# Bringing w_out in through the GpSimd DMA queue, cast to bf16 on the way

## The chip, the cores and the metric

The kernel runs on one core of one Trainium2 chip. The metric is the device time of one execution in microseconds (us). The core has five engines that run side by side: PE (TensorE, matrix multiplication), DVE (VectorE), ACT (ScalarE), POOL (GpSimd) and SP (SyncE, which here only issues DMAs). Sixteen DMA engines move data between HBM and the on-chip memory SBUF. PE writes its sums to PSUM, a small memory of eight banks.

## The reference

Sliding-window attention with a few global keys, followed by a feed-forward layer with softplus. Four sequences of 768 rows, 8 heads of 64; 96 local keys and 8 global ones; a feed-forward layer from 512 to 2048 and back.

```python
scores = scale * np.matmul(q, k.transpose(0, 1, 3, 2))
keep = is_global | is_local
scores = scores - slopes[:, None, None] * dist[None, :, :]
scores = np.where(keep, scores, -1000000000.0)
a = np.exp(scores - np.max(scores, axis=-1, keepdims=True))
a = a / (np.sum(a, axis=-1, keepdims=True) + 1e-09)
x = np.matmul(a, v)                        # heads side by side: 3072 x 512
h = x @ w_in                               # 512 x 2048
g = np.maximum(h, 0.0) + np.log1p(np.exp(-np.abs(h)))
return g @ w_out                           # 2048 x 512, float32
```

All inputs are float32 in HBM: q, k and v 6.3 MB each, w_in and w_out 4.2 MB each.

## The kernel before

**Tiles.** The 3072 rows are 24 blocks of 128 rows; two neighbouring blocks form a unit, for which q, k and v are loaded together (0.5 MB each). Two blocks also form a group of 256 rows in the feed-forward layer, so there are 12 units and 12 groups.

**Attention of a block n, in two parts of four heads.** q and k are cast to bf16 (`cast_q`, L718, or `cast_rows`, L737) and transposed, for the first three units on PE through PSUM (`transp_pe`, L803), later by transposing DMAs (`transp_dma`, L837). `scores` (L874) multiplies them into PSUM. For blocks in `PE_BIAS` PE first writes the distance bias into the bank (a seed, L887); for the others DVE adds it (`z`, L932). ACT takes the exponential into `pb` (L939), PE multiplies by v (L956), DVE divides by the row sum (L966, L967), and the result is transposed into `XT` (L986 to L998). From the third block of a sequence on, POOL copies the global keys and values beside the local ones (L854, L863).

**Feed-forward of a group g.** `mm1` (L1004) works in eight slots p of eight matmuls each: a slot needs both `XT` halves and its columns of `w_in_bf`. ACT takes exp (L1028, `e`) and ln(1 + e) (L1039, `g`). `mm2` (L1055) multiplies g by `w_out_bf`; a matmul with 256 rows of w_out needs piece p of eight. DVE copies the sum out and SP stores it.

**Weights.** `load_w` (L693) brings w_in and w_out in eight pieces of 0.5 MB each: SP issues a DMA into a float32 buffer of a ring of 12 (`raw`, L710), and an engine named in `ENG_W` casts it into `w_in_bf` or `w_out_bf` (L712). A raw buffer can be filled again only when its casts are done. A w_in piece holds half of the rows of 512 columns, so a slot waits for two pieces; pieces whose column index stands in `NARROW` hold all rows of 256 columns, so a slot waits for one.

**Order.** All operations are handed to a planner (L24 to L186), which is run when the program is built. It knows an estimated duration for each operation and each DMA, gives every operation a due time, worked backwards from the matmuls (`due`, L66, plus a shift from the table `NUDGE`), and plays the machine forward (`run`, L79), each engine taking the most urgent operation that is ready. The order that results is fixed for each engine. `FIRST_LOADS` (L190) is the order in which the raw buffers of the first three units and of the weights are handed out. Where PE would idle at the beginning, up to 90 matmuls on a blank tile are put in (`filler`, L1171); they compute nothing that is used.

**Queues.** SP issues nearly all DMAs, in one order; ACT issues q of the first unit and one store. POOL issues none. A DMA also waits until the one eight before it in the plan is done. In the order built, SP's loads stand as k0, v0, q1, k1, w_in 3, v1, w_in 1, 2, 7, 0, 6, 5, 4, q2, w_out 0, k2, v2, w_out 1, 3, 2, 4, 6, 7, 5 (k1's second half follows w_in 3), and then those of the fourth unit.

Of the kernel before, what the change touches and what calls it, by code (L numbers as in the profile page):

```python
# [23 lines left out]
class Planner:  # L24
# [54 lines left out]
    def run(self, first=0.7, dma_first=1.0, dma_last=1.4, fixed=None, stretch=None):  # L79
# [40 lines left out]
        while True:  # L120
# [50 lines left out]
            while events and events[0][0] <= now + 1e-9:  # L171
                _, _, kind, o = heapq.heappop(events)
                if kind == "free":
                    free[o.eng] = True
                    if o.work:
                        queues[o.eng].append([o, o.work * stretch(o), now + dma_first])
                    else:
                        o.end = now
                        tell([u for u in o.users if u.eng == o.eng])
                        push(now + o.lat, "done", o)  # L180
                else:
                    o.done = True
                    tell([u for u in o.users if o.work or u.eng != o.eng])
# [6 lines left out]
FIRST_LOADS = "v0 k0 q0 i3 i1 q1 o0 v1 k1 i0 i2 i7 i4 o1 i6 q2 k2 i5 o5 o2 o3 o7 v2 o6 o4".split()  # L190
LOAD_LEAD = 2.5
LEADS = {3: 2.25, 4: 2.75, 5: 3, 6: 2.75, 7: 2.75, 8: 3.5, 9: 2.25, 10: 2.75, 11: 3.5}
FILLERS = 90
TABLE_RANK = -9000.0
BIAS0_ON = ["ACT", "DVE"]
BIASA_ON = ["ACT"]
PE_BIAS = (0, 1, 3)
PE_KEYS = {
    0: (("s", 1, 0), ("s", 1, 1), ("h1",), ("o",)),
    1: (("s", 0, 0), ("s", 0, 1), ("s", 1, 0), ("s", 1, 1)),  # L200
    2: (("s", 1, 0), ("x",), ("s", 0, 0), ("s", 0, 1)),
}
PE_X = {0: ("h0",), 1: ("h0",), 2: ("o",), 3: ("o",), 4: ("x",), 5: ("x",)}
PV_KEYS = {
    (0, 0): ("o",),
    (0, 1): ("o",),
    (1, 0): ("o",),
    (1, 1): ("h1",),
# [6 lines left out]
    (0, 0): ("s", 0, 0),  # L215
# [7 lines left out]
NARROW = (0,)  # L223
TAIL = 8.0
ENG = {
    0: {"k": ["POOL", "DVE"], "q": ["POOL", "ACT"], "tk": ["DVE", "ACT"], "tq": ["DVE", "DVE"], "v": ["POOL"]},
    1: {"k": ["DVE", "POOL"], "q": ["POOL", "DVE"], "tk": ["ACT", "DVE"], "tq": ["DVE", "DVE"], "v": ["POOL", "DVE"]},
    2: {"k": ["ACT", "DVE"], "q": ["POOL", "POOL"], "tk": ["DVE", "DVE"], "tq": ["DVE", "DVE"], "v": ["POOL", "ACT"]},
}
ENG_X = {0: "DVE", 1: "ACT", 2: "DVE", 3: "DVE", 4: "ACT", 5: "ACT"}  # L230
ENG_W = {
    "i0": "DVE",
    "i1": "POOL",
    "i2": "POOL",
    "i3": "DVE",
    "i4": "POOL",
    "i5": "POOL",
    "i6": "POOL",
    "i7": "POOL",
    "o0": "POOL",  # L240
    "o1": "POOL",
    "o2": "DVE",
    "o3": "POOL",
    "o4": "POOL",
    "o5": "POOL",
    "o6": "POOL",
    "o7": "POOL",
# [3 lines left out]
    "a0.1": -1,  # L251
    "a0.2": 2,
    "a0.5": 1,
    "a0.6": -1,
    "a0.7": 0.5,
    "a1.0": -2,
    "a1.1": -1,
    "a1.3": -2,
    "a1.4": -2,
    "a1.5": 4,  # L260
    "a1.6": 2,
# [3 lines left out]
    "b0.0.0": 8,  # L265
    "b0.0.10": 0.5,
    "b0.0.14": 0.5,
    "b0.0.4": 0.5,
    "b0.0.6": -8,
    "b0.0.8": -1,  # L270
    "b0.1.0": 1,
    "b0.1.10": 1,
    "b0.1.12": 1,
    "b0.1.2": -8,
    "b0.1.8": -8,
    "b1.0.0": -0.5,
# [3 lines left out]
    "b1.0.2": -1,  # L280
# [7 lines left out]
    "biasFalse0": -1,  # L288
    "biasFalse1": -2,
    "biasFalse2": 0.5,  # L290
    "biasFalse3": -2,
    "biasFalse4": -2,
    "biasFalse5": 4,
    "biasFalse6": -4,
    "biasFalse7": -2,
    "biasTrue0": 1,
    "biasTrue1": -4,
    "biasTrue3": 2,
    "biasTrue4": 4,
    "biasTrue6": 0.5,  # L300
    "biasTrue7": 2,
    "castk0.1": -8,
    "castk1.0": 1,
    "castk1.1": 4,
    "castk2.0": 8,
    "castk2.1": 1,
    "castk3.00": -0.5,
    "castk3.10": -0.5,
# [3 lines left out]
    "castq0.0": 1,  # L312
    "castq0.1": 0.5,
    "castq1.1": -1,
    "castq2.0": -4,
    "castq2.1": 8,
    "castq4.0": 8,
    "castv0.00": -4,
    "castv0.11": -0.5,
    "castv1.00": -8,  # L320
    "castv1.01": 2,
    "castv1.11": -2,
    "castv2.00": 0.5,
    "castv2.01": -0.5,
    "castv2.10": 8,
    "castv2.11": -8,
# [5 lines left out]
    "cin1": 2,  # L332
    "cin2": -1,
    "cin3": 4,
    "cin4": -2,
    "cout0": -2,
    "cout1": 1,
    "cout3": -0.5,
    "cout5": -1,
    "cout6": -4,  # L340
    "cpk0.0": -1,
    "cpk0.1": 2,
    "cpk1.0": 0.5,
    "cpk2.1": 1,
    "cpq0.0": 0.5,
    "cpq0.1": 8,
    "cpq1.0": 1,
    "cpq2.0": 0.5,
    "cpq2.1": 8,
    "d0": 0.5,  # L350
    "d0e": 2,
    "dl0a": 2,
    "dl0b": 0.5,
    "dl0c": 8,
    "dl1a": 8,
    "dl1c": 8,
    "e0.1": 4,
    "e0.3": 2,
    "e0.5": 1,
    "e0.7": -8,  # L360
    "e1.0": -8,
    "e1.2": 8,
    "e1.4": -8,
    "e1.5": -1,
    "e1.6": -4,
# [4 lines left out]
    "ex1.0": 1,  # L370
    "ex1.1": -1,
    "ex2.0": -2,
    "ex3.1": 8,
    "ex4.1": -1,
    "ex5.0": -0.5,
    "ex5.1": 1,
    "gk5": -8,
    "gk7": 0.5,
    "gv4.0": -0.5,
    "gv4.1": 8,  # L380
    "gv5.0": 1,
    "gv5.1": 2,
    "gv6.0": -8,
    "gv6.1": 4,
    "gv7.0": 2,
    "gv8.0": -8,
    "gv8.1": -0.5,
    "ldk0.0": 1,
    "ldk0.1": -1,
    "ldk1.0": 8,  # L390
    "ldk1.1": -0.5,
    "ldk2.0": 2,
    "ldk4": 8,
    "ldk5": 0.5,
    "ldq0.0": -0.5,
    "ldq0.1": 8,
    "ldq1.0": 2,
    "ldq2.0": 0.5,
    "ldq2.1": 2,
    "ldq3": -4,  # L400
    "ldv1": 8,
    "ldv2": 8,
    "ldv4": 0.5,
# [3 lines left out]
    "ln0.0": -1,  # L407
    "ln0.1": 1,
    "ln0.3": -2,
    "ln1.0": 2,  # L410
    "ln1.1": 0.5,
    "ln1.3": -4,
    "nm0.0": -0.5,
    "nm0.1": -1,
    "nm1.0": -0.5,
    "nm2.1": -1,
    "nm3.0": 0.5,
    "nm4.0": 0.5,
    "nm4.1": -0.5,
    "nm5.0": -4,  # L420
    "nm5.1": 8,
# [3 lines left out]
    "oc0.1.0": -0.5,  # L425
    "oc1.0.0": 2,
    "ones": 4,
    "pv0.1": -8,
    "pv1.0": -8,
    "pv1.1": -1,  # L430
    "pv2.0": -2,
    "pv3.0": -1,
    "pv4.1": 8,
    "pv5.0": 8,
    "pv5.1": 8,
    "pv6.0": -1,
    "pv6.1": -4,
    "sb1.0": 1,
    "sb1.1": -0.5,
    "sb2.0": -2,  # L440
    "sb3.0": -2,
    "sb4.0": 1,
    "sb4.1": -4,
    "sc0.1": -4,
    "sc1.0": 8,
    "sc1.1": 0.5,
    "sc2.0": -0.5,
    "sc3.0": -8,
    "sc4.0": -0.5,
# [5 lines left out]
    "st0.1.0": -1,  # L455
    "st1.0.0": -4,
    "table": -1,
    "trk0.0": -8,
    "trk2.0": 0.5,
    "trk2.1": 2,  # L460
    "trk3": 0.5,
    "trk4": -2,
    "trq0.0": -4,
    "trq1.0": -0.5,
    "trq1.1": -2,
    "trq2.0": 2,
    "trq3": -0.5,
    "trq4": 8,
    "win0": 8,
    "win1": 8,  # L470
    "win2": -1,
    "win3": -2,
    "win4": -2,
    "win5": 8,
    "win6": 0.5,
    "win7": -8,
# [6 lines left out]
    "xc0": 2,  # L483
    "xc1": 8,
    "xc2": -1,
    "xc3": -2,
    "xc4": -1,
    "xc5": -4,
    "xt1": -1,
    "xt2": 1,  # L490
    "xt3": 2,
    "xt4": 1,
    "xt5": 0.5,
    "z4.0": 1,
    "z4.1": 0.5,
# [4 lines left out]
DIST0_ON = "ACT"  # L500
# [10 lines left out]
    (4, 1): 1,  # L511
    (5, 0): 1,
    (5, 1): 1,
    (6, 0): 0,
    (6, 1): 1,
    (7, 0): 1,
    (7, 1): 0,
}
T0 = 11.0
LATER = 55.0  # L520
MARGIN = {-1: 10.5, 0: -15.0, 1: 69.0, 2: 65.5, 3: 21.0}
SOONER = {"cin": -20.0, "cout": -25.0}
LAST_KEYS = (("s", 0, 0), ("x",), ("o",))
WHOLE = (0, 4, 6, 7, 8, 9, 10, 12, 13, 14, 15, 16, 17, 18, 23)
LOAD_ON = {"q0": "ACT"}


@with_exitstack
def kernel(
# [122 lines left out]
    def raw_slot(name):  # L652
        raw_of[name] = len(raw_of) % NRAW
        return raw_of[name]
# [38 lines left out]
    def load_w(which, p, rank, eng):  # L693

        slot = raw_slot((which, p))
        half, c = p % 2, p // 2
        raw = raw_t[slot][:].rearrange("p (a c) -> p a c", a=2)
        cost, issue = (1.37, 86.0), 0.45
        if which == "in" and c in NARROW:
            raw = raw_t[slot][:].rearrange("p (a c) -> p a c", a=NM)  # L700
            src = moe_w_in[:, W * p : W * p + W]
            dst = w_in_bf[:, :, W * p : W * p + W]
            cost, issue = (1.51, 51.0), 1.05
        elif which == "in":
            src = moe_w_in[W * half : W * half + W, 512 * c : 512 * c + 512]
            dst = w_in_bf[:, 2 * half : 2 * half + 2, 512 * c : 512 * c + 512]
        else:
            src = moe_w_out[W * p : W * p + W, :]
            dst = w_out_bf[:, 2 * p : 2 * p + 2, :]
        op(f"w{which}{p}", "SP", issue, rank, lambda: nc.sync.dma_start(raw, src.rearrange("(a p) c -> p a c", p=P)),  # L710
           writes=raw_keys(slot), dma=cost)
        op(f"c{which}{p}", eng, t_copy(eng, 1024, True), rank, lambda: copy_on[eng](dst, raw),  # L712
           reads=raw_keys(slot), writes=[("w" + which, p)], port=eng == "DVE")
# [71 lines left out]
    def kt_of(n):  # L785
        return kt_unit(unit_of(n))[:, n % 2, :, :]
# [86 lines left out]

    def scores(n, parts, rank):  # L874
# [70 lines left out]
    def pv(n, part, key, rank):  # L945
        i = blocks[n][1]
        u_all = 2 if i else 1
        pb, xs = pb_t[(2 * n + part) % NPB], xs_t[n % NXS]
# [4 lines left out]
        def mm():  # L953
            for h in range(4):
                for u in range(u_all):
                    nc.tensor.matmul(  # L956
                        xv[:, h, :], pb[:, u_all * (2 * (h % 2) + h // 2) + u, :],
                        vb_of(prev if u else n)[:, 4 * part + h, :], start=u == 0, stop=u == u_all - 1,
                    )

        reads = [("pb", (2 * n + part) % NPB), "ones"] + v_keys(n) + (v_keys(prev) if i else [])
# [232 lines left out]
    def attend(n, rank):  # L1194
# [4 lines left out]
        for parts in ((0, 1),) if n in WHOLE else ((0,), (1,)):  # L1199
            scores(n, parts, rank + 0.1 * parts[0])  # L1200
            for part in parts:
                soften(n, part, rank + 0.1 * part)
# [137 lines left out]
```

The softmax here doesn't subtract the row's maximum and nothing guards it: scores larger than these inputs give would overflow.

## Time and profile before

| what | value |
|---|---|
| runs | 222.47, 222.72, 223.34, 222.39 us |
| median | 222.59 us |
| the profiled execution | 222.47 us, of which 220.4 us is the span of the engines' work |
| DMA bytes | 40.96 MB in 220.4 us; HBM read 27.26 MB, written 6.29 MB |
| first feed-forward matmul (L1013) | starts at 22.88 us |
| casts of w_out (L712) | POOL x7, 1042 ns each; DVE x1, 682 ns |
| w_out DMA (L710), issue by SP | x8, median 440 ns |

The span runs from the first to the last instruction of the engines; what lies around it (222.47 - 220.4 = 2.07 us) belongs to the start and the end of the execution. In the profile an engine followed by q (SPq, POOLq) is its queue that issues DMAs and waits. PEld is the loading of weights into PE, beside its multiplications. In a timeline a bracket behind an instruction tells how long the engine had been idle and what ended that.

### The profile page before, as it was taken

What the parts mean: (1) busy time and instruction counts of PE and PEld (TensorE: products, weight loads), DVE (VectorE), ACT (ScalarE), POOL (GpSimd) and SP (SyncE); (2) the same over time, 40 slices, a digit from 0 to 9 for tenths busy, and PEclk for the clock granted to TensorE, in tenths of its full rate; (3) what the DMA queues carried; (4) which work ended last, traced back from release to release, by engine and by line L of the source; (5) the groups of instructions that cost most, each with busy time, mean ns of one, the idle gap of its engine ahead of it and who ended that gap; (6) DMA issues with size and microseconds to landing.
All of it is one profiled execution on the core that took longest, in us unless ns stands there. A gap on an engine that the chain in (4) does not pass through costs nothing.

```text
span 220.4 us, 5042 instructions
## 1 busy us (share of the span) xinstructions
PE 214.5 (97%) x2034; PEld 151.1 (69%) x2062; DVE 111.2 (50%) x204; ACT 160.1 (73%) x216; POOL 92.4 (42%) x156
## 2 busy tenths in 40 slices
PE   8999999999999999999999999999999999999994
PEld 5877896666676876667667757756657777767554
DVE  6469466644676567338447348347448642001121
ACT  5553999936889798678788688678689678887300
POOL 4557776788461576913962402126602220000000
PEclk9999999999999999999999999999999999999999
DMA  5999999999999798999993241999921222011112
GB/s 199 322 346 379 382 360 384 290 266 226 253 237 233 202 239 211 205 247 291 135 183 106 51 141 54 184 248 301 164 60 51 48 74 71 3 48 48 42 57 95
DMA packets 70359, 40.96 MB, mean 186 GB/s; under 512 B 30144, under 2 KB 62272, under 8 KB 70336
## 3 DMA queue, kind: packets, MB, share of 16 engines
q1 hardware_dynamic: 69904, 40.05, 71.9%
q10 hardware_dynamic: 432, 0.59, 0.9%
q8 instruction: 16, 0.26, 0.5%
q14 instruction: 7, 0.06, 0.1%
HBM read 27.26 MB, written 6.29 MB: 152 GB/s over the span
## 4 chain that ended last, share of the span: by engine, by line
PE 82%; DMA 11%; ACT 3%; SPq 2%; issue 1%; DVE 0%; ACTq 0%
PE h_ps L1013 35%; PE o_ps L1062 30%; PE s_ps L1062 5%; PE s_ps L906 5%; PE x_ps L956 5%; DMA raw<-in_moe_w_in_dram 4%; DMA raw<-in_k_dram 4%; DMA raw<-in_v_dram 3%; PE x_ps L1062 2%; SPq L710 2%; ACT e L1028 1%; ACT g L1039 1%; SPq L675 1%; ACT vb L754 1%; ACT kb L730 0%
## 5 line engine op out<-in xcount | busy, mean ns | idle before, releaser
L1013 PE MATMUL h_ps<-XT,w_in_bf 128*128 128x256 bf16 x768 | 95.8, 273 | 0.4 <-ACT e L1028 0.2
L1013 PEld LDWEIGHTS <-w_in_bf 128*128 128x128 bf16 x768 | 72.8, 98 | 17.4 <-issue 0.4
L1028 ACT ACTIVATE e<-h_ps 128x512 f32<-128x512 f32 x96 | 60.0, 630 | 31.7 <-PE h_ps L1013 31.3
L1062 PE MATMUL o_ps<-w_out_bf,g 128*128 128x512 bf16 (+1 forms) x296 | 74.1, 371 | 1.2
L1062 PEld LDWEIGHTS <-g 128*128 128x128 bf16 x416 | 37.4, 98 | 29.4
L932 DVE TENSOR_TENSOR z<-s_ps,biasA 128x1024 f32<-128x1024 f32 x36 | 43.2, 1217 | 17.8 <-PE s_ps L906 11.2
L1039 ACT ACTIVATE g<-e 128x1024 bf16<-128x1024 f32 x48 | 50.7, 1057 | 1.4
L939 ACT ACTIVATE pb<-z 128x1024 bf16<-128x1024 f32 (+1 forms) x42 | 41.1, 987 | 4.1 <-DVE z L932 4.0
L754 POOL CAST kb<-raw 64x512 bf16<-64x512 f32 x36 | 23.2, 645 | 24.2 <-DMA raw<-in_k_dram 22.9
L863 POOL COPY vb<-vb 4x512 bf16<-4x512 bf16 x32 | 20.0, 625 | 30.8 <-PE x_ps L956 29.9
L754 POOL CAST vb<-raw 64x512 bf16<-64x512 f32 x44 | 27.3, 621 | 13.2 <-DMA raw<-in_v_dram 11.4
L1091 DVE COPY osb<-o_ps 128x512 f32<-128x512 f32 (+1 forms) x20 | 13.4, 670 | 38.3 <-PE o_ps L1062 38.0
L956 PEld LDWEIGHTS <-pb 128*128 128x128 bf16 x352 | 16.6, 98 | 5.8
L966 DVE RECIPROCAL rcp<-x_ps 128x4 f32<-128x4 f32 x40 | 7.1, 178 | 23.2 <-PE x_ps L956 23.0
L967 DVE TENSOR_TENSOR xs<-x_ps,rcp 128x256 bf16<-128x256 f32 x40 | 17.0, 424 | 1.4
L956 PE MATMUL x_ps<-vb,pb 128*128 128x65 bf16 x304 | 15.9, 193 | 0.0
L1174 PE MATMUL x_ps<-blank 128*128 128x256 bf16 x90 | 14.3, 318 | 1.1 <-DVE blank L1113 1.1
L1062 PE MATMUL s_ps<-w_out_bf,g 128*128 128x512 bf16 (+1 forms) x62 | 13.1, 351 | 0.1
L1174 PEld LDWEIGHTS <-blank 128*128 128x128 bf16 x90 | 9.8, 115 | 3.6 <-DVE blank L1113 1.1
L906 PEld LDWEIGHTS <-kT 64*128 64x128 bf16 x224 | 6.8, 94 | 6.1 <-issue 5.7
L906 PE MATMUL s_ps<-qT,kT 64*128 64x128 bf16 x224 | 10.5, 218 | 0.0
L712 POOL CAST w_out_bf<-raw 128x1024 bf16<-128x1024 f32 x7 | 7.3, 1041 | 3.3 <-DMA raw<-in_moe_w_out_dram 3.3
(72 smaller groups left out, 105.0 us busy)
## 6 DMA issues: line engine op xcount, KB each, us to landing
raw<-in_v_dram SPq DMA_DIRECT2D x12, 512.0 KB, 5.5
out_dram<-osb SPq DMA_DIRECT2D x23, 256.0 KB, 2.6
raw<-in_q_dram SPq DMA_DIRECT2D x9, 512.0 KB, 5.2
raw<-in_k_dram SPq DMA_DIRECT2D x9, 512.0 KB, 5.3
raw<-in_moe_w_in_dram SPq DMA_DIRECT2D x8, 512.0 KB, 9.8
raw<-in_moe_w_out_dram SPq DMA_DIRECT2D x8, 512.0 KB, 9.1
raw<-in_k_dram SPq DMA_DIRECT2D x6, 256.0 KB, 6.3
raw<-in_q_dram SPq DMA_DIRECT2D x4, 256.0 KB, 8.4
```

What stands on the lines that cost most here:

```text
L754: copy_on[eng](dst, src)
L863: nc.gpsimd.tensor_copy(vb_of(prev)[sl, :, 0:D], vb_of(first)[sl, :, 0:D])
L906: nc.tensor.matmul(reg if unit_of(n) in WIDE else reg.rearrange("p (r t) -> p r t", r=2), kt[rows, 2 * part + m, :], qv(rows, 2 * part + m ...
L932: nc.vector.tensor_tensor(z, src, bias, ALU.add)
L939: nc.scalar.activation(pb[:, 0:nr, :].rearrange("p (y a) b -> p y (a b)", y=2), src, AF.Exp, scale=1.0 / root_d)
L956: nc.tensor.matmul(xv[:, h, :], pb[:, u_all * (2 * (h % 2) + h // 2) + u, :], vb_of(prev if u else n)[:, 4 * part + h, :], start=u == 0, s ...
L967: nc.vector.tensor_tensor(xs[:, 4 * part : 4 * part + 4, :], xv[:, :, 0:D], rcp[:][:, :, None].to_broadcast([P, 4, D]), ALU.mult,)
L1013: last = nc.tensor.matmul(hv[:, j, :], w_in_bf[:, m, fb * P : fb * P + P], XT[g % NXG][:, m, :], start=(m == 0), stop=(m == NM - 1),)
L1028: nc.scalar.activation(e[:, p % 2, :, :].rearrange("p j (b t r) -> p (j b) r t", b=2, r=2), hb[:].rearrange("p (a r t) -> p a r t", a=4, r=2),
L1039: nc.scalar.activation(gt[:, 2 * p - 2 : 2 * p + 2, :].rearrange("p a t -> p (a t)"), e[:].rearrange("p a j t -> p (a j t)"), AF.Ln, bias=1.0,
L1062: nc.tensor.matmul(bank(key)[:, 0 : z - a], gt[:, fb, ns * P : ns * P + P], w_out_bf[:, fb, a:z], start=(fb == 0), stop=(fb == NFB - 1),)
L1174: nc.tensor.matmul(x_ps[:, 0:256], blank[:, 0:P], blank[:, 0:256])
```

## The change

The eight loads of w_out no longer go through raw buffers. POOL issues a DMA whose source is float32 rows in HBM and whose destination is the bf16 tile `w_out_bf`, so that the DMA engines convert. The eight SP issues, the eight casts and the eight turns in the ring of raw buffers are gone. The planner's clock has a longer start for a DMA that POOL issues (1.8 us added), 0.55 us for its issue and 1.55 us for its work.

```diff
-                        queues[o.eng].append([o, o.work * stretch(o), now + dma_first])
+                        queues[o.eng].append([o, o.work * stretch(o), now + dma_first + 1.8 * (o.eng == "POOL")])
...
-        slot = raw_slot((which, p))
         half, c = p % 2, p // 2
-        raw = raw_t[slot][:].rearrange("p (a c) -> p a c", a=2)
+        slot = None
+        if which == "in" or p not in CAST_OUT:
+            slot = raw_slot((which, p))
+            raw = raw_t[slot][:].rearrange("p (a c) -> p a c", a=2)
...
+        if which == "out" and p in CAST_OUT:
+            op(f"cout{p}", "POOL", 0.55, rank, lambda: nc.gpsimd.dma_start(dst, src.rearrange("(a p) c -> p a c", p=P)),
+               writes=[("wout", p)], dma=(1.55, 86.0))
+            return
...
+CAST_OUT = (0, 1, 2, 3, 4, 5, 6, 7)
```

With it come other settings of the plan: the order of the first loads, which engine casts what, which blocks get their bias on PE, in which PSUM banks things stand, and many entries of `NUDGE` (not shown).

```diff
-FIRST_LOADS = "v0 k0 q0 i3 i1 q1 o0 v1 k1 i0 i2 i7 i4 o1 i6 q2 k2 i5 o5 o2 o3 o7 v2 o6 o4".split()
+FIRST_LOADS = "q0 v0 k0 i3 k1 q1 o5 i2 k2 i1 o3 v1 i7 o7 i6 o0 o1 q2 i4 o6 i0 o4 o2 v2 i5".split()
-BIAS0_ON = ["ACT", "DVE"]
+BIAS0_ON = ["DVE"]
-PE_BIAS = (0, 1, 3)
+PE_BIAS = (0, 1, 2)
-NARROW = (0,)
+NARROW = ()
 ENG = {
-    0: {"k": ["POOL", "DVE"], "q": ["POOL", "ACT"], "tk": ["DVE", "ACT"], "tq": ["DVE", "DVE"], "v": ["POOL"]},
-    1: {"k": ["DVE", "POOL"], "q": ["POOL", "DVE"], "tk": ["ACT", "DVE"], "tq": ["DVE", "DVE"], "v": ["POOL", "DVE"]},
-    2: {"k": ["ACT", "DVE"], "q": ["POOL", "POOL"], "tk": ["DVE", "DVE"], "tq": ["DVE", "DVE"], "v": ["POOL", "ACT"]},
+    0: {"k": ["ACT", "POOL"], "q": ["POOL", "ACT"], "tk": ["DVE", "DVE"], "tq": ["ACT", "DVE"], "v": ["POOL", "DVE"]},
+    1: {"k": ["DVE", "POOL"], "q": ["POOL", "ACT"], "tk": ["DVE", "ACT"], "tq": ["DVE", "ACT"], "v": ["POOL"]},
+    2: {"k": ["DVE", "DVE"], "q": ["DVE", "POOL"], "tk": ["ACT", "DVE"], "tq": ["DVE", "ACT"], "v": ["ACT"]},
 }
...
-DIST0_ON = "ACT"
+DIST0_ON = "POOL"
...
-T0 = 11.0
-LATER = 55.0
-MARGIN = {-1: 10.5, 0: -15.0, 1: 69.0, 2: 65.5, 3: 21.0}
-SOONER = {"cin": -20.0, "cout": -25.0}
+T0 = 55.0
+LATER = 45.0
+MARGIN = {-1: 10.5, 0: 3.0, 1: 54.0, 2: 91.0, 3: 15.0}
+SOONER = {"cin": -11.0, "cout": -32.0}
-WHOLE = (0, 4, 6, 7, 8, 9, 10, 12, 13, 14, 15, 16, 17, 18, 23)
+WHOLE = (4, 6, 8, 9, 10, 11, 12, 13, 15, 16, 17, 18, 20, 22, 23)
 LOAD_ON = {"q0": "ACT"}
+LONE = ()
```

The diff also brings a second way to score a block (`scores_lone`), used for blocks named in `LONE`; that is empty, so nothing calls it.

In the order that the changed program has, SP's loads stand as k0, v0, q1, k1, q2 (first half), v1, k2 (first half), q2 (second half), w_in 3, k2 (second half), w_in 1, 0, 2, 5, 4, 6, 7, v2, and then the fourth unit. POOL's issues of w_out stand as 0, 2, 1, 4, 3, 5, 6, 7: 0 ahead of the copy of the distance tile (`dist0`), 2 behind the cast of q1, 1 behind the cast of w_in 0, 4 behind that of w_in 2, 3 and 5 behind that of w_in 5, 6 and 7 behind that of w_in 7. PE's order from the first feed-forward matmul is, for the first group: slots 0 to 3 with attention between them, slots 4 and 5, four matmuls of mm2 (w_out 0 and 1), slot 6, two of mm2 (w_out 2), slot 7. Before, all eight slots and three of the second group stood ahead of the first matmul of mm2.

## The prediction

> **What bounds the kernel now.** I read the page first: busy shares, the slices, the chain of waits.
>
> ```profile
> PE 214.5 (97%) x2034; PEld 151.1 (69%) x2062; DVE 111.2 (50%) x204; ACT 160.1 (73%) x216; POOL 92.4 (42%) x156
> ...
> DMA  5999999999999798999993241999921222011112
> ...
> PE 82%; DMA 11%; ACT 3%; SPq 2%; issue 1%; DVE 0%; ACTq 0%
> ```
>
> PE carries 82% of the chain. The 11% of DMA all lies in the chain's first 30 us, where the DMA row is full too. So there are two regimes, and I asked for busy time in stretches cut at the first feed-forward matmul (22.88 us). Columns: length, busy time of PE, PEld, DVE, ACT and POOL, granted clock, DMA share, GB/s.
>
> ```profile
> 1.00:22.88 21.88, 21.56 (x211) 16.90 (x214) 15.18 (x35) 12.21 (x25) 12.13 (x20) 1.00 0.99 328
> 22.88:36.30 13.42, 13.05 (x150) 11.58 (x147) 8.04 (x16) 12.66 (x19) 10.35 (x14) 1.00 1.07 375
> 36.30:60.00 23.70, 23.49 (x227) 15.34 (x231) 12.36 (x22) 17.30 (x23) 16.93 (x26) 1.00 1.10 267
> ```
>
> PE looks full everywhere, but before 22.88 much of it is filler: matmuls on a blank tile (L1174), 85 of the 90. PE's timeline shows where real work becomes dense (start, length, work).
>
> ```profile
> 18.06 1.47 PE L1174 MATMUL x_ps<-blank 128*128 128x256 bf16 x12
> ...
> 22.88 1.92 PE L1013 MATMUL h_ps<-XT,w_in_bf 128*128 128x256 bf16 x16
> ...
> 24.77 0.49 PE L1174 MATMUL x_ps<-blank 128*128 128x256 bf16 x3
> ...
> 33.01 0.38 PE L1174 MATMUL x_ps<-blank 128*128 128x256 bf16 x2
> ```
>
> After 22.88 five fillers are left, and PE never idles long. The end is therefore "first feed-forward matmul, plus the PE work left, plus later stalls": 217.6 - 22.88 = 194.7 us of it now. What can move the time is what fills the first 36 us, and there the DMA engines move 375 GB/s without a break. Since nothing compresses that stream, I read landing times from POOL's timeline: a cast whose bracket names a DMA began as its bytes landed.
>
> ```profile
> 23.12 1.04 POOL L712 CAST w_in_bf<-raw 128x1024 bf16<-128x1024 f32 x1 [0.83 <-DMA raw<-in_moe_w_in_dram]
> 24.47 1.04 POOL L712 CAST w_in_bf<-raw 128x1024 bf16<-128x1024 f32 x1 [0.31 <-DMA raw<-in_moe_w_in_dram]
> ...
> 25.83 1.04 POOL L712 CAST w_in_bf<-raw 128x1024 bf16<-128x1024 f32 x1 [0.16 <-DMA raw<-in_moe_w_in_dram]
> ...
> 33.08 1.04 POOL L712 CAST w_out_bf<-raw 128x1024 bf16<-128x1024 f32 x1 [0.16 <-DMA raw<-in_moe_w_out_dram]
> 34.37 1.04 POOL L712 CAST w_out_bf<-raw 128x1024 bf16<-128x1024 f32 x1 [0.25 <-DMA raw<-in_moe_w_out_dram]
> ...
> 37.05 1.04 POOL L712 CAST w_out_bf<-raw 128x1024 bf16<-128x1024 f32 x1 [1.48 <-DMA raw<-in_moe_w_out_dram]
> 38.37 1.04 POOL L712 CAST w_out_bf<-raw 128x1024 bf16<-128x1024 f32 x1 [0.28 <-DMA raw<-in_moe_w_out_dram]
> ```
>
> Counting 0.5 MB slots along SP's order (with q0 on ACT's queue) these are 6.0, 6.5, 7.0, 9.5, 10.0, 11.0 and 11.5 MB. So 6.5 MB are down at 24.5 us, 9.5 at 33.1, and each slot costs about 1.35 us. All of w_in is down at 25.8 us; q2, k2, v2 and seven of the eight w_out transfers follow it.
>
> **What the Trainium skill says.** "DMA: Bandwidth & Descriptors", section "SWDGE vs HWDGE vs iDMA": a casting DMA can only be issued from GpSimd, where software writes its descriptors. No queue here is of that kind, so no run yet shows the cost. The same page, "Issuing engines are not separate DMA queues": transfers of all issuers share the same 16 engines and interleave. The trace agrees as far as it can: ACT's queue and SP's together stay near one rate (359 GB/s from 3 to 6 us). Its "Queues, rings and completion order" adds that an engine takes turns between rings that hold work. That one I rely on, untested here. "SBUF — State Buffer", "Who interferes with whom": descriptor writing waits while VectorE copies or casts in a two-port mode. VectorE is busy 15.2 of the first 21.9 us, with tensor_scalar and casts among it; again no run shows the size.
>
> **The change part by part.** *Removed:* eight SP issues and eight casts of w_out, seven on POOL at 1.04 us (7.3 us) and one on DVE (0.68 us). They lie between 28.5 and 42.1 us, and the chain of waits holds none of them, so they are worth nothing directly. *Bytes:* HBM is still read for 4 MB of w_out; only the SBUF side halves. The bound is a read rate or a write rate; if the latter, each transfer falls from 1.35 to about 0.7 us. I take 1.35, bounds 0.7 and 2.0 (cast slower than copy).
>
> *Added on POOL:* eight issues. No row shows one. From below, an SP issue of w_out takes 0.44 us (median); from above, a POOL cast of the same tile, 1.04. I take 1.0, since software writes as many rows. The issues stand in POOL's order as follows: w_out 0 ahead of the copy that starts the bias tiles, w_out 2 after the q1 cast, w_out 1 after the cast of w_in 0, w_out 4 after that of w_in 2, then 3 and 5, then after the w_in 7 cast 6 and 7. Behind the first are only the bias tiles: even 1 us late they are done near 6.5 us (0.22 us each on DVE), while the first transposes come at 7.94 now. That one is covered.
>
> *Moved, and it decides:* SP now carries q2 and k2 before w_in. By its order w_in 0 is the slot that ends at 5.5 MB, with w_out 0 and 2 also issued early: 6.5 MB, 24.5 us (6.0 MB, 23.1, if the casting transfers cost half). Its cast on POOL, 1.04 us, comes straight before the first matmul that needs it (both half slices are needed now, as no slice is narrow). That gives 24.2 to 25.5 us; I take 25.2, against 22.88.
>
> What PE has done by then is more: 12 more transposes (0.104 us each, 1.25), four more probability-times-v matmuls (0.15), and all 90 fillers, where five (0.71 from the starts around them) came later. So 2.1 us less is left: 192.6. Equal times therefore mean a first matmul at 25.0; 25.2 costs 0.2. The bias seed moves from a wide block to a narrow one; that saving of some 0.35 us is ahead of the first matmul and hidden by the fillers.
>
> *What is late next:* the last w_in slices. From the first feed-forward matmul to slot 6, PE's order holds six slots of 0.87 (5.24), four mm2 matmuls of 0.216 (0.86), and attention of 1.87 (16 score matmuls 0.55, 16 value matmuls 0.70, transposes 0.62): 7.97 us, so slot 6 is due at 33.2. It needs w_in 6 and 7. SP's stream up to w_in 7 is 8.0 MB, plus w_out 0 and 2 (9.0), plus what w_out 1, 4, 3 take in turns from about 27 us on, where POOL has issued them: from 0.5 MB (9.5, 33.1 us) to an equal share until the end (about 35.5 us). I take 9.75 MB, 33.7 us; with POOL's cast 34.8. Stall 1.6 us, from 0.6 to 3.3. In the kernel now w_in is down at 25.8 and no such stall exists. A small wait at slot 4 (w_in 4 through DVE) is inside it.
>
> *After that:* PE work is the same; the reordering of the rest can win at most the idle left, 1.4 us (lengths less busy time after 36.3, modelled ends), or lose about 1. I take 0. v2 is cast on ACT, four times 0.62 us, due near 41: covered unless v2 lands after 38.
>
> *Sum:* 192.6 + 25.2 + 1.6 = 219.4, against 217.6: +1.8. The profiled execution is 222.47 (span 220.4, 2.07 around it), so 224.3. Its median stands 0.12 higher, within the spread.
>
> **The rivals.** *Early mm2 pays.* w_in arrives in time, as transfers with halved writes take less; first matmul 24.2, stall 0.2, up to 0.5 us won in the steady part: 192.6 + 24.2 + 0.2 - 0.5 = 216.5, 221.4. For it: POOL is relieved by 7.3 us of casts, and mm2 matmuls stand earlier in PE's order. Against it: the DMA row is full, and the bytes read are unchanged. It decides once w_in 7 lands before 32 us. *A draw:* a stall of 0.2 us after a first matmul at 25.0, about 222.7. *Casting transfers are slow* (2.0 us each, or starved of descriptor time): six of them before w_in 7 and v2, 0.65 us each, 3.9 us beyond the forecast less about 1 us of slack there: 227.2. For it: nothing here shows such a queue. Against: the removed casts leave POOL time. *The change does not do what it says* (rows staged anyway): the built order shows eight issues into the w_out tile and no cast of it, so I give that nothing.
>
> **How the numbers follow.** Forecast case (first matmul near 25, stall 0.6 to 3.3): 0.47. Early mm2 pays: 0.23. Draw: 0.15. Slow casting transfers: 0.15. About 0.3% (0.67 us) is what a measurement of this kernel can tell from no change. The forecast case spans 223.0 to 226.0; its lowest edge, 0.02 of the chance, lies within the bound. Faster 0.23, same 0.17, slower 0.60. To leave no more than 2 in 10 out, the range takes half of the faster case and part of the slow one: 221.5 to 227.3.
>
> **What would show it.** Right: DMA full to about 40 us; first feed-forward matmul between 24.2 and 25.5; a PE gap of 1 to 3 us before slot 6 of the first group, ended by a POOL or DVE cast of w_in that itself waited for its DMA; no cast of w_out. Wrong: w_in 7 down before 32 us; casting transfers that land in half the time, or in twice it; POOL issues far from 1 us; or a PE stall elsewhere, such as at the v2 casts or in the steady part.

## The result, and the profile after

| | before | after |
|---|---|---|
| median | 222.42 us (222.05 to 223.34, 17 runs) | 224.30 us (222.95 to 225.16, 12 runs) |
| profiled execution, span | 222.47, 220.4 us | 224.98, 223.0 us |
| first feed-forward matmul | 22.88 us | 26.36 us |
| end of PE's last matmul | 217.61 us | 220.05 us |

The ratio is 1.0079 (95% interval 1.0059 to 1.0098): the changed kernel is slower by 1.9 us. Its profiled execution lies 0.68 us above its own median, that of the kernel before 0.05, so the two traces differ by more (2.5 us) than the medians do.

From the page of the kernel after: the busy times, the DMA row of the slices, the queues, the chain of waits by engine, and the issue of w_out (KB written, median us from issue to landing).

```profile
PE 213.9 (96%) x2033; PEld 150.6 (68%) x2062; DVE 110.5 (50%) x207; ACT 161.8 (73%) x216; POOL 88.1 (40%) x155
...
DMA  5999999999998787889921795795691222011112
...
q1 hardware_dynamic: 67216, 35.86, 64.4%
q0 software_dynamic: 2176, 2.10, 5.9%
...
PE 81%; DMA 9%; ACT 6%; DVE 2%; issue 1%; DVEq 0%
...
w_out_bf<-in_moe_w_out_dram POOLq DMA_DIRECT2D x8, 256.0 KB, 8.0
```

POOL has lost 4.3 us of work and PE has as much as it had; neither shows in the time. q0 is the new queue: eight casting transfers, counted by the 2.10 MB that they write; they read twice that. Its share, 5.9% of 223.0 us of 16 engines, is 1.64 us for each.

The same stretches as before, cut at the first feed-forward matmul.

```profile
1.00:26.36 25.36, 23.14 (x233) 18.23 (x235) 15.22 (x40) 14.01 (x25) 15.09 (x25) 1.00 0.96 298
26.36:36.30 9.94, 9.89 (x116) 8.01 (x116) 6.98 (x14) 8.97 (x14) 7.73 (x12) 1.00 1.14 283
36.30:60.00 23.70, 22.21 (x202) 15.50 (x204) 11.22 (x18) 19.04 (x27) 11.46 (x20) 1.00 1.19 232
```

From 26.36 to 36.30 PE is idle for 0.05 us, so the stall that was expected there is absent. From 36.30 to 60.00 it is idle for 1.49 us (0.21 before). PE's timeline shows both the late start and the place of the late stall; the bracket gives the idle time ahead and what ended it.

```profile
12.84 0.29 PE L997 MATMUL h_ps<-vb,pb 128*128 128x65 bf16 x4 [1.00 <-ACT biasA L1192]
...
25.97 0.60 PE L815 MATMUL s_ps<-ident,qb 128*128 128x128 bf16 x4 [0.84 <-DVE z L971]
26.36 1.08 PE L1055 MATMUL h_ps<-XT,w_in_bf 128*128 128x256 bf16 x8
...
34.31 1.04 PE L1055 MATMUL h_ps<-XT,w_in_bf 128*128 128x256 bf16 x8
...
42.17 1.46 PE L1104 MATMUL s_ps<-w_out_bf,g 128*128 128x512 bf16 x6
44.97 0.40 PE L997 MATMUL x_ps<-vb,pb 128*128 128x65 bf16 x8 [1.33 <-DVE xs L1009]
```

The line at 34.31 is slot 6 of the first group, which doesn't wait. The stall is at 44.97: the second value product of block 4 waits for the division (`xs`) of its first, whose bank it shares. The first line matters below: PE stands idle for 1.00 us ahead of block 0's first value product. Its bracket names the last of ACT's bias tiles, but POOL's first cast of v0 (0.86 us from 11.92, further down) ends 0.06 us ahead of it; which of the two it was is settled below. DVE's timeline says why the division was late.

```profile
43.67 0.69 DVE L730 CAST qb<-raw 128x1024 bf16<-128x1024 f32 x1 [3.82 <-DMA raw<-in_q_dram]
44.28 0.17 DVE L1008 RECIPROCAL rcp<-x_ps 128x4 f32<-128x4 f32 x1
44.49 0.42 DVE L1009 TENSOR_TENSOR xs<-x_ps,rcp 128x256 bf16<-128x256 f32 x1
```

DVE stood idle for 3.82 us with the cast of q3 (q of the fourth unit) at the head of its order, until q3 landed at 43.67; the division stands behind it. In the kernel before the division came first (43.67) and the cast of q3 followed at 44.01 without a wait. q3 is one of the loads that SP issues behind w_in, now side by side with w_out. It isn't much later than before: there SP issued it at 34.15 and it landed 8.6 us later, at 42.75, but nothing urgent stood behind its cast. POOL's timeline gives the issues of w_out and the last w_in piece.

```profile
2.21 0.84 POOL L707 DMA_DIRECT2D w_out_bf<-in_moe_w_out_dram  x1
...
11.92 1.62 POOL L754 CAST vb<-raw 64x512 bf16<-64x512 f32 x2 [4.95 <-DMA raw<-in_v_dram]
...
24.89 1.04 POOL L712 CAST w_in_bf<-raw 128x1024 bf16<-128x1024 f32 x1 [0.30 <-DMA raw<-in_moe_w_in_dram]
25.88 0.72 POOL L707 DMA_DIRECT2D w_out_bf<-in_moe_w_out_dram  x1
...
29.29 1.48 POOL L707 DMA_DIRECT2D w_out_bf<-in_moe_w_out_dram  x2
32.25 1.04 POOL L712 CAST w_in_bf<-raw 128x1024 bf16<-128x1024 f32 x1 [1.48 <-DMA raw<-in_moe_w_in_dram]
```

An issue holds POOL for 0.72 us in the median. w_in 0 is cast at 25.93, w_in 7 at 33.29. v0, which landed at 8.40 before, lands at 11.92: w_out 0, issued at 2.21, runs beside it.

**Where the time went, by PE alone.** With 192.6 us of PE work left after the first feed-forward matmul, 26.36 us gives 218.96; the trace ends at 220.05, so 1.09 us are stalls after it. Against the 217.61 before, 1.36 us come from the late start (26.36 less the equal-time point of 25.0) and 1.09 from the late stall. (PE's bracket says 1.33. In kernels without this stall PE waits 0.24 us for ACT at the next slot instead, in `q3_late` at 43.67; that wait is part of the 192.6.)

### The profile page after: what moved, and what is told of

It is laid out like the page before. It is cut to its first block, busy times and chain, and to the rows that moved or that the text cites. A ratio compares the mean times of both kernels' runs of the same rounds, so it can differ in the third digit from the quotient of the medians.

```text
span 223.0 us, 5036 instructions
## 1 busy us (share of the span) xinstructions
PE 213.9 (96%) x2033; PEld 150.6 (68%) x2062; DVE 110.5 (50%) x207; ACT 161.8 (73%) x216; POOL 88.1 (40%) x155
## 3 DMA queue, kind: packets, MB, share of 16 engines
q0 software_dynamic: 2176, 2.10, 5.9%
## 4 chain that ended last, share of the span: by engine, by line
PE 81%; DMA 9%; ACT 6%; DVE 2%; issue 1%; DVEq 0%
PE h_ps L1055 32%; PE o_ps L1104 28%; DMA raw<-in_q_dram 9%; PE x_ps L1216 4%; PE s_ps L945 4%; PE x_ps L997 4%; PE s_ps L1104 3%; ACT pb L978 2%; PE x_ps L1104 2%; ACT g L1081 1%; ACT e L1070 1%; PE s_ps L815 1%; ACT biasA L1192 1%; DVE z L971 1%; PE s_ps L926 1%
## 5 line engine op out<-in xcount | busy, mean ns | idle before, releaser
L971 DVE TENSOR_TENSOR z<-s_ps,biasA 128x1024 f32<-128x1024 f32 x38 | 45.8, 1218 | 14.9 <-PE s_ps L945 11.5
L978 ACT ACTIVATE pb<-z 128x1024 bf16<-128x1024 f32 (+1 forms) x42 | 41.9, 1008 | 7.5 <-DVE z L971 7.5
L754 POOL CAST kb<-raw 64x512 bf16<-64x512 f32 x36 | 22.3, 620 | 30.3 <-DMA raw<-in_k_dram 28.9
L754 POOL CAST vb<-raw 64x512 bf16<-64x512 f32 x42 | 26.3, 625 | 19.7 <-DMA raw<-in_v_dram 13.9
L997 PEld LDWEIGHTS <-pb 128*128 128x128 bf16 x352 | 16.6, 98 | 8.9 <-issue 1.9
L1008 DVE RECIPROCAL rcp<-x_ps 128x4 f32<-128x4 f32 x40 | 7.2, 180 | 25.1 <-PE x_ps L997 24.9
L997 PE MATMUL x_ps<-vb,pb 128*128 128x65 bf16 x304 | 15.8, 193 | 1.4 <-DVE xs L1009 1.3
L1216 PE MATMUL x_ps<-blank 128*128 128x256 bf16 x90 | 13.6, 307 | 1.1 <-DVE blank L1155 1.1
L730 DVE CAST qb<-raw 128x1024 bf16<-128x1024 f32 (+1 forms) x10 | 7.1, 714 | 4.9 <-DMA raw<-in_q_dram 4.9
```

Source lines behind the costliest of these rows:

```text
L754: copy_on[eng](dst, src)
L971: nc.vector.tensor_tensor(z, src, bias, ALU.add)
L978: nc.scalar.activation(pb[:, 0:nr, :].rearrange("p (y a) b -> p y (a b)", y=2), src, AF.Exp, scale=1.0 / root_d)
L997: nc.tensor.matmul(xv[:, h, :], pb[:, 4 * (h % 2) + 2 * part + h // 2 if lone else u_all * (2 * (h % 2) + h // 2) + u, :], vb_of(prev if u ...
L1216: nc.tensor.matmul(x_ps[:, 0:256], blank[:, 0:P], blank[:, 0:256])
```

## The experiments

A first theory, A, put the late stall on q3's cast in front of the divisions. A second, B, asked whether the first feed-forward matmul is late because of w_in 0 or because of PE's own order. The rivals: the casting path itself is dear, or POOL's issues are.

### q3's cast behind the divisions (`q3_late`)

The order that the planner returns is changed by hand: the cast of q3 (`castq3.0`) and its transposing DMA go behind the division of block 4's second half (`nm4.1`).

```diff
     order = pl.run()
+    for name, behind in [('castq3.0', 'nm4.1'), ('trq3', 'castq3.0')]:
+        o = next(x for x in order if x.name == name)
+        order.remove(o)
+        order.insert(1 + [x.name for x in order].index(behind), o)
```

> Only the cast of the fourth unit's q on DVE, and the transposing DMA that reads it, stand behind the two divisions of block 4 instead of ahead of them; every other order is that of the changed kernel. Theory (in the changed kernel DVE waits 3.8 us for q3 to land, and the division behind it stops PE for 1.3 to 1.5 us near 43.5 to 45.0): that stall goes, nothing else moves, about 223.0 us, 1.3 less than 224.3. Rival (q3 is late for whoever needs it, the wait is only paid at the next consumer): 224.3.

Measured: 223.11 us (222.50 to 224.34, 20 runs), ratio to the kernel before 1.0031 (1.0017 to 1.0046). This interval lies wholly below that of the changed kernel. PE's timeline of this kernel:

```profile
33.12 1.35 PE L1055 MATMUL h_ps<-XT,w_in_bf 128*128 128x256 bf16 x8
...
41.05 0.41 PE L997 MATMUL x_ps<-vb,pb 128*128 128x65 bf16 x8
41.30 1.46 PE L1104 MATMUL s_ps<-w_out_bf,g 128*128 128x512 bf16 x6
42.59 0.41 PE L997 MATMUL x_ps<-vb,pb 128*128 128x65 bf16 x8
...
46.35 0.37 PE L997 MATMUL x_ps<-vb,pb 128*128 128x65 bf16 x7 [0.53 <-POOL vb L863]
```

The two value products of block 4 follow each other with only the mm2 matmuls between them: the stall is gone, and the median is 1.2 us lower (1.1 if each kernel is compared with the runs of the kernel before that were taken beside it). So A is shown: a late landing reached PE through the order of DVE, not through w_in. In this one execution, though, two other waits took the gain back (from the first feed-forward matmul to the end it needs 193.66 us, the changed kernel 193.69); a second trace of the same kernel, below, has neither of them. Slot 6 (33.12) now comes 1.19 us earlier and takes 1.35 us for eight matmuls that take 1.04 elsewhere: w_in 7 was cast at 33.58, so the stall forecast for slot 6 is there once PE is early enough, at 0.31 us. And at 46.35 PE waits 0.53 us for POOL's copies of global values, which stood behind the cast of k3, landed at 44.47.

### The bytes taken away (`tiny`)

Each w_out transfer brings 64 of its 512 columns; mm2 has as many matmuls of the same size, on those columns again and again.

```diff
-            op(f"cout{p}", "POOL", 0.55, rank, lambda: nc.gpsimd.dma_start(dst, src.rearrange("(a p) c -> p a c", p=P)),
+            op(f"cout{p}", "POOL", 0.55, rank, lambda: nc.gpsimd.dma_start(dst[:, :, 0:64], src.rearrange("(a p) c -> p a c", p=P)[:, :, 0:64]),
...
-                        w_out_bf[:, fb, a:z],
+                        w_out_bf[:, fb, None, 0:64].to_broadcast([P, (z - a) // 64, 64]),
```

> Each w_out transfer brings 64 of 512 columns and the second product reads these 64 over and over, so most of w_out is left out of the computation; orders, waits and matmul counts are those of the changed kernel. It takes some seven eighths of the casting transfers' load off the DMA engines. Theory A (the first feed-forward matmul is held by w_in 0, which waits behind two w_out transfers): it starts near 23.5 us instead of 26.4 and the q3 stall goes too: about 220.3. Theory B (it is held by PE's order, fillers and the bias addition ahead of it, and contention only makes q3 late): first matmul stays at 25.5 to 26.4, only the stall of 1.3 goes: about 222.8. Rival (the DMA path has no part in the loss): 224.3.

Measured: 222.49 us (222.22 to 223.16, 12 runs), ratio 1.0007 (0.9991 to 1.0023): no difference from the kernel before can be seen. The issues and the number of q0's packets (2176) are those of the changed kernel, and its order is the same. So neither POOL's issues nor the new order loses time by itself; the 1.8 us between the two medians are what the bytes of w_out do to other loads in this order (in the order of `q3_late` the same bytes cost 1.1 us less). Views of both kernels, the changed one first, show it: the queues from 28 to 46 us (packets, MB, share of 16 engines' time), then the load of q3 from 24 to 28 us (KB, and us from the start of its issue to its landing).

```profile
q1 hardware_dynamic: 5046, 3.10, 64.7%
q0 software_dynamic: 1632, 1.57, 51.6%
...
raw<-in_q_dram SPq DMA_DIRECT2D x1, 512.0 KB, 20.1
```

```profile
q1 hardware_dynamic: 5247, 2.37, 55.4%
q0 software_dynamic: 1380, 0.17, 15.1%
...
raw<-in_q_dram SPq DMA_DIRECT2D x1, 512.0 KB, 12.9
```

The same loads in three kernels (k3 and v3 are the fourth unit's too), each in us from the start of its issue to its landing (SP's issue of q3 was itself held for 4.8 us in the changed kernel and for 4.3 in this one):

| load | before | changed kernel | small transfers |
|---|---|---|---|
| v0 | 6.0 | 9.7 | 6.2 |
| q3 | 8.6 | 20.1 | 12.9 |
| k3 | 8.3 | 16.8 | 8.3 |
| v3 | 8.6 | 11.6 | 6.2 |

How the two queues share the engines in the changed kernel shows from 31 to 40 us, with about as many packets for each but larger ones for q0:

```profile
q0 software_dynamic: 1264, 1.22, 79.8%
q1 hardware_dynamic: 1466, 0.76, 38.7%
```

For B, this kernel's POOL and PE:

```profile
20.77 2.10 POOL L712 CAST w_in_bf<-raw 128x1024 bf16<-128x1024 f32 x2
```

```profile
25.30 0.60 PE L815 MATMUL s_ps<-ident,qb 128*128 128x128 bf16 x4 [0.84 <-DVE z L971]
25.70 1.08 PE L1055 MATMUL h_ps<-XT,w_in_bf 128*128 128x256 bf16 x8
```

w_in 0 is cast by 22.87 us, and the first feed-forward matmul still waits until 25.70. So it isn't w_in 0 that holds it: B's PE order does, with the waits for DVE's bias addition (`z`) that stand in it (here 0.84 us).

### The same again (`q3_again`), and k3's cast moved too (`k3_late`)

The first of k3's casts on POOL is put behind the two copies of global values; the kernel with q3's cast moved is run once more as its base.

```diff
+    pool = [x for x in order if x.eng == "POOL"]
+    at = next(i for i, x in enumerate(pool) if x.name == "castk3.00")
+    order.remove(pool[at])
+    order.insert(1 + order.index(pool[at + 2]), pool[at])
```

> The kernel of q3_late once more, on the chip of k3_late, as its base. Theory: 223.1 us within 0.3, ratio to the kernel before 1.003; PE's wait of about 0.5 us for the copies of global values near 46.4 is there again. Rival: the head of the program, which varied by 1.2 us between executions, sets the time, and the median moves by more than 0.5 us.

> q3_late, and in POOL's order the first of the four casts of k3 (L754) moved behind the two copies of global values (L863) that stood after it. Theory (a late landing stalls PE through whatever stands behind its cast in an engine's order): in q3_late k3 landed at 44.5 us, its cast stood in front of the copies, and PE waited 0.53 us at 46.35 for them. With the cast behind them that wait goes, the median falls by up to 0.5 us to 222.6 to 223.0, beside q3_again of the same call. Rival (PE has slack there in another wait): the next wait, on the same block's divisions or on k3's transposes, takes its place and the median stays within 0.2 us of q3_again.

Measured: 223.29 us (22 runs), ratio 1.0041 (1.0027 to 1.0054), for the base, and 223.18 (22 runs), 1.0037 (1.0021 to 1.0053), with k3 moved. The extra move brings nothing that can be seen. The base's trace shows why: in this execution k3 landed at 43.31, and the wait of 0.53 us wasn't there to be won. The first run's wait was one execution's, and my expectation had taken it for a fixed cost.

The traces settle B, though. The table takes from PE's timelines the first transposes, the first value product of block 0 (L997), the first feed-forward matmul (mm1), the end of PE, and from POOL's the landing of v0.

| kernel | first transposes | v0 lands | value product | mm1 | mm1 less product | PE ends | end less mm1 |
|---|---|---|---|---|---|---|---|
| changed kernel | 7.20 | 11.92 | 12.84 | 26.36 | 13.52 | 220.05 | 193.69 |
| q3 moved | 7.02 | 10.67 | 11.58 | 25.11 | 13.53 | 218.77 | 193.66 |
| q3 moved, again | 7.87 | 9.21 | 12.34 | 25.87 | 13.53 | 218.47 | 192.60 |
| q3 and k3 moved | 7.18 | 11.84 | 12.75 | 26.28 | 13.53 | 218.87 | 192.59 |
| small transfers (`tiny`) | 7.70 | 8.33 | 12.17 | 25.70 | 13.53 | 218.29 | 192.59 |

The first feed-forward matmul stands 13.5 us behind block 0's first value product in all five, wherever w_in 0 lands: a rigid stretch of PE's order, with waits for DVE of 0.17 and 0.84 us in it. From that matmul on PE needs 192.6 us, or 1.1 more where waits are left: the division in the changed kernel, w_in 7 and k3's cast in the first trace with q3 moved.

What varies is the start of the stretch. In three of the kernels the value product comes 0.91 to 0.92 us after the landing of v0, in the other two, where v0 lands by 9.3, 4.47 us after PE's first transposes. So v0 it is, and not ACT's bias tiles: in the first trace with q3 moved the product runs ahead of the tiles that the bracket names.

```profile
11.58 0.29 PE L997 MATMUL h_ps<-vb,pb 128*128 128x65 bf16 x4
11.63 1.03 ACT L1192 ACTIVATE biasA<-dist 128x256 bf16<-128x256 f32 x3
```

Against the 4.47 us the late v0 costs 1.17, 0.09 and 1.10 us. But where v0 is late the first transposes are early (7.0 to 7.2 for 7.7 to 7.9), so the first feed-forward matmul is at 25.1 to 26.4 beside full transfers and at 25.7 beside small ones. The spread of executions from 222.95 to 225.16 us thus has a cause at hand in the head, though single executions without a trace can't be put down to it. It stays open how the 0.6 to 0.8 us by which the median with q3 moved (223.11, 223.29) lies above that of `tiny` (222.49) divide between v0 and the other loads.

### The head shortened

Beside q3's cast, three of the w_out issues (`cout`) and the transposes of q2 and k2 (`trq`, `trk`, with their copies) are moved behind later work, and of the 90 fillers the last 36 are dropped (`best1`), none (`best2`), or every second of those 36 (`best3`, with two more moves). `nofill` is the changed kernel with only the 36 dropped. The edit of `best1`, whose second part alone is `nofill` and whose first alone is `best2`:

```diff
+    for name, behind in [('castq3.0', 'nm4.1'), ('trq3', 'castq3.0'), ('cout0', 'cin1'), ('cout2', 'cin2'), ('cout4', 'cout3'), ('trq2.0', 'a0.1'), ('cpq2.0', 'trq2.0'), ('trk2.0', 'a0.2'), ('cpk2.0', 'trk2.0')]:
...
+    order = [o for o in order if not (o.name.startswith("fill") and int(o.name[4:]) >= 54)]
```

> The changed kernel's orders without the last 36 filler matmuls (all that stand behind the first value product). Theory (the first feed-forward matmul is held by PE's own order: fillers ahead of ready work, then the bias addition of block 3 on DVE and the q2 transposes behind it): it moves up from 26.4 by 0.5 to 1.2 us; until then w_in 0 (cast done at 25.9) binds it too. Together 0.5 to 1 us less than 224.3. Rival (w_in 0 alone holds it): 224.3.

> All of it in one: q3's cast behind the divisions of block 4; no fillers behind the first value product; w_out 0 and 2 issued behind the casts of w_in 1 and 2 instead of at the start and behind q1, w_out 4 behind w_out 3; the q2 transposes that wait for block 3's bias addition, with their copy, behind slot 1 of the first group, and the last k2 transposes behind slot 2. Theory (first matmul held by PE's order, w_in 0 and the q2 transposes together; late stall by q3): first matmul near 23.5 to 24.3, no stall near 44: 220.8 to 221.6, faster than both kernels. Rival (w_out issued later comes too late for the second product, or v2 and q3 are pushed back further): no better than 223.

> The moves of best1 with all 90 fillers kept. Theory (best1 started its feed-forward at 23.2 but lost it to a lower PE clock once the fillers were gone): the clock stays at full speed, the first feed-forward matmul is held by PE's order with fillers and comes at 24.2 to 25.2, no stall of PE near 44: 221.6 to 222.6. Rival (the moves themselves cost, w_out and q3 late): 223.5 as best1.

> As best2, with every second of the last 36 fillers left out and the first half of the k2 transposes, with its copy, behind slot 0. If the remaining 18 fillers keep the PE clock up, the first feed-forward matmul comes at 23.2 to 24.2: 220.8 to 221.8. If they don't, the clock falls in a slice near 20 us as in best1 and nofill, the early slots take longer: 223 or more.

| kernel | median | ratio to before |
|---|---|---|
| nofill | 223.35 (222.90 to 224.99, 10 runs) | 1.0025 (1.0005 to 1.0045) |
| best1 | 223.64 (222.98 to 225.31, 9 runs) | 1.0060 (1.0035 to 1.0086) |
| best2 | 224.50 (224.34 to 225.27, 6 runs) | 1.0096 (1.0070 to 1.0122) |
| best3 | 224.90 (224.46 to 228.78, 7 runs) | 1.0114 (1.0081 to 1.0147) |

None is faster than the kernel before, and `best1` and `best2` miss the ranges expected of them by about 2 us. `best2` keeps the clock and shows what the moves do to PE:

```profile
24.16 1.03 PE L1055 MATMUL h_ps<-XT,w_in_bf 128*128 128x256 bf16 x8
26.31 0.38 PE L1028 MATMUL o_ps<-ident,xs 128*128 128x128 bf16 x4 [1.11 <-DVE xs L1009]
...
29.12 0.40 PE L997 MATMUL o_ps<-vb,pb 128*128 128x65 bf16 x8 [1.11 <-DVE XT L1033]
```

The matmul comes 2.2 us earlier than in the changed kernel, and two waits of 1.11 us for DVE take that back; that the moved work had covered them is my reading. The four moved transposes of q2, 0.4 us, still have to be done behind it. In `best1`, where w_out 0 is issued later and the fillers are gone, w_in 0 at last holds the first matmul, and in this execution the clock is the next cost:

```profile
23.16 1.84 PE L1055 MATMUL h_ps<-XT,w_in_bf 128*128 128x256 bf16 x8 [0.63 <-POOL w_in_bf L712]
...
25.22 1.75 PE L1055 MATMUL h_ps<-XT,w_in_bf 128*128 128x256 bf16 x8
```

Its page's clock row has a 6 in the fifth slice (22 to 28 us), and eight matmuls take 1.84 us for 1.08. `nofill` alone shows the same in its profiled execution:

```profile
PEclk9998599999999999999999999999999999999999
```

In that trace the first feed-forward matmul comes at 26.94, later than in the changed kernel and not earlier, as had been expected. The median of `nofill` is nevertheless about 1 us below the changed kernel's (intervals 1.0005 to 1.0045 and 1.0059 to 1.0098). The clock doesn't sort its executions: its mean over an execution was at most 0.992 in seven of the ten, and six of these took 222.90 to 223.75 us, the three at full clock 222.90 to 224.09; only the profiled one (0.984, 224.99) stands out. In `best1` the mean was below 0.999 only in the two slowest of nine (0.992 and 0.983; 225.31 and 224.96), so the clock can explain these two at most, not the median. Why `nofill` is faster than the changed kernel stays open. The trace of `best3` is of its slowest execution, 228.78 us, and isn't used.

### What a casting transfer costs

In `plain4` four of the eight transfers bring float32 into a float32 tile uncast, and mm2 reads the upper halves of those numbers. In `half_plain` all eight bring 256 of the 512 columns uncast, with this edit (that of `plain4` is of the same kind, for pieces 0, 1, 2 and 4):

```diff
-    w_out_bf = const.tile([P, NFB, DM], BF16, name="w_out_bf")
+    w_out_f = const.tile([P, NFB, DM // 2], F32, name="w_out_f")
...
-            op(f"cout{p}", "POOL", 0.55, rank, lambda: nc.gpsimd.dma_start(dst, src.rearrange("(a p) c -> p a c", p=P)),
+            op(f"cout{p}", "POOL", 0.55, rank, lambda: nc.gpsimd.dma_start(w_out_f[:, 2 * p : 2 * p + 2, :], src.rearrange("(a p) c -> p a c", p=P)[:, :, 0:256]),
...
+                        w_out_f[:, fb, :].bitcast(BF16)[:, None, 1:256:2].to_broadcast([P, (z - a) // 128, 128]),
```

> Four of the eight w_out pieces (0, 1, 2, 4) come through POOL's queue without a cast, 2 KB rows into a float32 tile of their own, whose upper halves the second product reads; the other four are cast as before. In the changed kernel the queue's packets took 5.9% of 16 engines' span, 1.64 us for a piece. If the cast makes a transfer dear, the queue's share falls to about 5.4% (1.37 us for a plain piece); if the queue itself does, it stays at 5.9%.

> Each w_out piece brings 256 of 512 columns as float32 without a cast, 1 KB read and 1 KB written for each row, and the second product reads the upper halves of 128 of them over and over; most of w_out is left out of the computation. If a casting piece is priced by what it reads (2 KB a row), the queue's share falls from 5.9 to about 3%; if by what it writes (1 KB) or by packets, it stays near 5.9%.

Measured: 224.82 and 226.14 us, one run each. These times are no comparison, since mm2's matmuls on every second bf16 take longer (378 and 379 ns for 371; half_plain has 384 of them). The queue's lines are what was wanted, first of `plain4`, then of `half_plain`.

```profile
q0 software_dynamic: 1664, 3.15, 5.4%
```

```profile
q0 software_dynamic: 640, 2.10, 2.9%
```

5.4% of 222.8 us is 12.03 for four casting and four plain transfers; with 1.64 for a casting one, a plain one takes 1.36. A transfer of `half_plain` writes the 256 KB that a casting one writes, but reads 256 instead of 512: 0.81 us, half of 1.64. So the price follows the bytes that are read and not those written, and writing half of them wins nothing that can be seen. The number of packets doesn't set it either: `half_plain` has fewer of them too (640), but `tiny` has the 2176 of the changed kernel, and its 1.9% of 221.2 us are 0.53 us for a transfer. That is more than an eighth of 1.64, so the price isn't simply proportional where rows are short. The surcharge for casting is less sure: in `best1` and `best2` q0's share is 5.5%, or 1.54 us for a casting transfer; put in place of 1.64, that leaves 1.47 for a plain one. So the surcharge lies between some 5 and 20%.

### Plan and path exchanged

`after_hw` has the changed kernel's settings with w_out through SP again; `before_cast` has those of the kernel before with casting transfers. Both orders are planned anew.

```diff
-CAST_OUT = (0, 1, 2, 3, 4, 5, 6, 7)
+CAST_OUT = ()
```

and in `load_w` of the kernel before

```diff
+            op(f"cout{p}", "POOL", 0.55, rank, lambda: nc.gpsimd.dma_start(dst, src.rearrange("(a p) c -> p a c", p=P)),
+               writes=[("wout", p)], dma=(1.55, 86.0))
+            return
```

> The changed kernel's settings, but w_out loaded by SP as float32 and cast on chip; the planner orders the program anew. Theory (the casting transfers cost the time): 222.4 to 223.5, w_in down earlier. Rival (the settings of the plan cost it, whichever way w_out comes): 224.3 or more.

> The settings of the kernel before, but w_out through POOL's queue with the cast in the DMA; ordered anew. Theory (casting transfers are dearer than plain ones, 1.64 against 1.35 us, and push back the loads beside them): 223.5 to 225. Rival (the path itself is neutral or better, the new settings lose): 222.4 or less.

Measured: 234.22 us (4 runs), ratio 1.0511 (1.0444 to 1.0577), and 230.25 us (4 runs), 1.0361 (1.0323 to 1.0399). Neither tells the paths apart, since both are 8 to 12 us slower than the kernel before. In `after_hw` PE waits 3.31 us at one value product; in `before_cast` seven waits of 0.4 to 0.9 us lie between 30 and 41 us. The settings fit one path each, and a new plan costs more than the difference that was asked for. They show only that a path can't be exchanged without the tables that go with it.

## Why the prediction was right in its number, and where it was not

- **The sum** (+1.8, 224.3 us): measured +1.9, 224.3. Part of that is luck. In the trace the late start costs 1.36 us, for which 0.2 had been put down, and the late stall 1.09, for which 1.6 had been put down at another place and for another cause; one is too small, the other too large. The frame of the sum held: 192.6 us from the first feed-forward matmul to the end, found as 192.59 to 192.60 where nothing else stalls.
- **First matmul at 25.2:** measured 26.36 in the profiled execution, 25.1 to 26.4 over the five kernels of the table. The size was short by 1.2 us in that execution; the cause was wrong. The step that failed is "Its cast on POOL, 1.04 us, comes straight before the first matmul that needs it". The landing was right (24.89 for 24.5), and in the changed kernel the cast does end 0.04 us before the transposes that precede that matmul. But where the cast was done 2.8 us ahead of it (`tiny`), the matmul still stood at 25.70. What holds it is PE's order, 13.53 us from block 0's first value product, and in front of it v0, late behind w_out 0. I counted w_out 0 as bytes ahead of w_in and as an issue ahead of the bias tiles, not as a neighbour of v0.
- **Late stall of 1.6 us before slot 6:** 1.09 us, in another place. The step that failed is "9.75 MB, 33.7 us; with POOL's cast 34.8": w_in 7 landed at 32.25 (30.9 to 32.6 in the traces with q3 moved). With the start at 25.11 slot 6 did lose 0.31 us, so that mechanism is there but small. What I left out were the casts of q3 and k3, loads that SP issues last and that run beside the casting transfers, and where these casts stand in the orders of DVE and POOL; I looked at v2 alone for what comes after.
- **"After that: 0":** right where q3's cast was moved and nothing else stalled (`q3_again`, `k3_late`): end less first matmul 192.6.
- **POOL issue 1.0 us** (0.44 to 1.04): 0.72, and off the path, as the kernel with small transfers shows.
- **A casting transfer 1.35 us** (0.7 to 2.0): 1.54 to 1.64. The lower bound, a price by bytes written, is refuted by `half_plain`.
- **What the Trainium skill said:** "DMA: Bandwidth & Descriptors", section "Queues, rings and completion order", has an engine take turns between rings that hold work. The trace agrees: from 31 to 40 us, with loads of both queues under way throughout, q0 had 1264 packets and q1 1466, though q0 read 2.44 MB in them (1.22 written) and q1 moved 0.76. "SBUF — State Buffer", section "Who interferes with whom", has descriptor writing wait while VectorE works in a two-port mode: no run here separates such a cost; the eight issues took 716 to 843 ns each.
- **The rivals:** "Early mm2 pays" was to be decided by w_in 7 landing before 32 us; at 32.25 it stood at the edge, and what it missed was v0 and q3. Slow casting transfers were refuted at 2.0 us each, though in spirit this one was close: without the bytes of w_out the loss is gone (`tiny`). But the order has its part in it, since another place for one cast wins 1.1 us with all bytes there (`q3_late`).
- **A reading of the lines:** the 375 GB/s "without a break" hold from 22.88 to 36.30 us only; the row before that says 328.

Not tried is a w_out 0 issued later with nothing else moved. It was moved in `best1` and `best2`, where v0 landed at 8.5 and 8.9, but with other moves beside it.

## What to carry to other kernels

When a transfer moves to a queue of its own, ask which loads it now runs beside, and for each of these what stands behind its first use in the order of an engine: here more than half of the cost came through a cast that waited on DVE in front of a division. A converting DMA saves the engine's cast and the buffer, not the read; if the DMA engines are full, count it by its source. Before a late first matmul is put on the operand that lands last, look whether its distance to an earlier instruction of its own engine is fixed.

## What was not expected of the hardware

- A casting transfer of 0.5 MB into 256 KB took 1.54 to 1.64 us of the 16 engines' time, and one of 256 KB into 256 KB without a cast 0.81: at these row lengths the source decides.
- Loads of v, q and k beside the casting transfers were hit hard: q3 took 20.1 us from issue to landing for 12.9 beside small ones, k3 16.8 for 8.3. From 31 to 40 us the two queues had about as many packets each, and q0's were the larger ones.
- The MB and GB/s of the profile count a casting transfer by what it writes. From 28 to 46 us the page's view has 3.10 + 1.57 MB; by bytes read it is 6.24 MB in 18 us, 347 GB/s, so a fall of the GB/s row there isn't a fall of what HBM delivers.
- With 36 fillers dropped (`nofill`), the granted clock of PE fell to 0.5 of full speed in one slice of the profiled execution, and eight matmuls of 256 columns took 1.60 us for 1.08; other executions with a mean clock of 0.992 were no slower than those at full clock.
